# A linear-attention and SwiGLU kernel: first two chunks accumulated over all unit groups, loads limited to two in flight, last pair stored by halves, a new written order

## The chip, the cores and the metric

The kernel runs on one core of a Trainium2 chip. The metric is device time in microseconds (us); the kernel before took 604.38 us, the median of three runs (603.22 to 606.6). A change of about 0.5%, 3 us, is the least that runs of this kernel can tell from none. The engines are named as in the profile: PE multiplies matrices (PEld loads its stationary operand), DVE is the vector engine, ACT the scalar engine, POOL the third elementwise engine, SP the queue that issues most of the transfers (DMAs).

## The reference

Inputs are `r`, `k`, `v` of shape (4, 8, 768, 48), a decay `w` and a bonus `u` of shape (8, 48), and three FFN weights. Per batch and head, a state of 48 x 48 runs over 768 steps; its output is normalised and goes through a gated FFN (384 to 1536 to 384):

```python
for t in range(S):
    cur = einsum('bhd,bhe->bhde', u[None] * k_t, v_t)
    y[:, :, t] = einsum('bhd,bhde->bhe', r_t, state + cur)
    state = w[None, :, :, None] * state + einsum('bhd,bhe->bhde', k_t, v_t)
x = y.transpose(0, 2, 1, 3).reshape(B * S, H * D)
xn = x / sqrt(mean(x * x, axis=-1) + 1e-06) * rms_g
g = xn @ w_gate
out = (g * sigmoid(g) * (xn @ w_val)) @ w_out
```

## The kernel before, in words

**Tiling.** The 768 steps are cut into 12 chunks of 64; with 4 batches, a chunk is 256 tokens. `mixing(s)` (line 788) does the attention of chunk s: products of keys and queries ("E" for chunk 0, "A" later, tile names `chan,ku` and `RR,chan`), a masked copy `MT` on DVE, the outputs Y (`MT,V`, then `RX,ST` and `RR,ST`, which add the state's part), the state update U (`V,KH`), a row of squared sums r (`ones,sq`), and its spread as a diagonal (`diag,ones`). DVE, ACT and POOL build what lies between: decayed queries `RR`, decayed keys in `chan`, `KH`, the norm `ms` and `diag`, and `xa`, `xb`, which are the normalised chunk in two layouts.

**Weights.** They lie in DRAM as 64-bit floats. `quarter(i)` and `piece` (lines 380 to 419 and 972 to 982) load a piece into one of six `raw` buffers (SP), work the low bits on ACT (`ulp`) and DVE (`bits`), and sum on POOL into the 32-bit weights `wa` (gate), `wb` (value) and `wo` (second layer). There are four unit groups; each has two or three pieces of `wa` and of `wb` and two of `wo`, and in the kernel before a group's `wo` follows its `wa` and `wb`.

**The first two chunks** go through the FFN directly while the weights arrive. `gate_val` (line 994) makes one block of units for one chunk: a gate and a value product on PE (12 records each), then a silu on ACT and a multiplication on DVE into `h`. `cell(s, i)` (line 1044) does three such blocks; `add_cell` (line 1024) then projects one unit group through `wo` into a PSUM bank of its own, "P" in this text. The first group's result is copied by ACT into `rows_out`, the next three are added to it by DVE.

**The other ten chunks** go in five pairs. `group(s, m)` makes seven gate and value products for two chunks at a time out of sums of weights and of tokens, six times. `second_layer(s)` (line 1129) makes the projection of a pair out of seven blocks, P1 to P7, each of 24 records on PE, in five half banks: x and w are the two halves of bank a, y is in b, z and v are the halves of c. `plus` adds on DVE, `result` stores. `m1` is ACT's copy of P1's result, made after P1 and before P2 adds to the same half. For the last pair the stores are split between SP's queue and ACT's, and only P3, the last block, is made by halves of the tokens (`js`).

**Order.** Nothing is scheduled by the machine's arrival. Every operation is registered with `Plan.add` with an engine, a cost in us, and the keys that it reads and writes; then `Plan.give` issues all of them in the order of a list of numbers written at the top, `ORDER` (lines 83 to 155). `InOrder` (line 158) keeps that order on every engine; all its instructions have one line in the profile, L166. An engine thus waits at an operation until its inputs are there, with everything that follows queued behind it. `Plan.times` works a start time out of the costs; it is used only by `warm` (line 1082), which puts nine matmuls on ones ahead of the first real product.

**Transfers.** All loads go through SP's queue, in order. A load is issued as soon as SP reaches it and its buffer is free; there is no limit on the number under way. Looks at the raw weights (`check`, line 762) also load through SP, into `rows_out`, in the first and middle part, and count values that the fast path can't take.

**End.** `flag` (line 1203) sums these counts, copies the number into `bad` (DVE, after the last pair's second result row), and all engines load it (L1219) as their last act before a branch (`tc.If`, L1670) over a general kernel that isn't entered here. SP and ACT reach the load only after their last stores.

Of the kernel before, what the change touches and what calls it, by code (L numbers as in the profile page):

```python
# [49 lines left out]
P = 128  # L50
# [22 lines left out]
def feature_order():  # L73
# [10 lines left out]
    0, 5, 1, 14, 9, 4, 6, 49, 3, 16, 2, 19, 54, 11, 8, 17, 15, 12, 50, 51, 53, 24, 55, 10, 57, 52, 20, 56, 59, 29, 84,  # L84
    60, 34, 13, 58, 66, 61, 106, 18, 67, 63, 62, 21, 68, 22, 70, 31, 73, 32, 25, 74, 39, 26, 64, 27, 69, 85, 23, 75,
    65, 7, 91, 71, 76, 72, 28, 77, 109, 86, 96, 78, 139, 36, 44, 37, 79, 140, 142, 97, 114, 30, 87, 92, 80, 143, 88,
    93, 33, 90, 108, 98, 89, 141, 41, 119, 35, 101, 42, 45, 46, 40, 47, 144, 107, 94, 38, 147, 149, 129, 145, 150, 43,
    102, 146, 99, 134, 148, 48, 103, 151, 213, 104, 100, 95, 105, 152, 116, 175, 81, 110, 111, 153, 112, 117, 115,
    154, 113, 120, 155, 124, 176, 118, 156, 82, 222, 157, 171, 158, 83, 159, 166, 160, 216, 121, 167, 161, 122, 172,
    162, 123, 227, 185, 164, 126, 217, 173, 165, 125, 177, 127, 163, 214, 168, 136, 130, 128, 174, 170, 186, 250, 181,  # L90
    187, 218, 219, 182, 188, 131, 132, 178, 183, 135, 137, 259, 195, 184, 242, 247, 260, 179, 196, 248, 232, 180, 133,
    191, 197, 249, 215, 192, 198, 138, 256, 169, 205, 193, 229, 228, 273, 257, 189, 251, 308, 253, 230, 223, 194, 237,
    254, 220, 221, 190, 252, 255, 307, 206, 224, 225, 199, 207, 233, 258, 226, 200, 310, 231, 201, 261, 238, 202, 320,
    234, 208, 235, 274, 209, 354, 262, 210, 236, 211, 203, 275, 265, 266, 263, 212, 355, 357, 267, 358, 283, 268, 356,
    312, 239, 244, 204, 245, 276, 243, 240, 285, 311, 284, 330, 361, 380, 279, 315, 313, 280, 277, 241, 264, 293, 281,
    246, 363, 282, 309, 278, 294, 364, 317, 325, 314, 366, 289, 295, 316, 296, 414, 286, 269, 290, 322, 318, 303, 291,
    360, 292, 319, 359, 367, 326, 413, 362, 299, 331, 327, 328, 287, 304, 321, 365, 300, 323, 567, 301, 368, 305, 288,
    306, 302, 332, 369, 297, 270, 372, 370, 373, 568, 371, 570, 374, 335, 344, 375, 333, 569, 324, 298, 329, 376, 576,
    334, 383, 579, 415, 340, 381, 337, 571, 382, 341, 385, 346, 342, 336, 343, 338, 347, 593, 350, 348, 345, 339, 600,
    580, 384, 351, 387, 388, 393, 352, 353, 394, 377, 349, 400, 395, 577, 396, 390, 401, 272, 412, 404, 402, 271, 403,  # L100
    405, 574, 626, 416, 379, 445, 378, 627, 572, 573, 417, 599, 406, 397, 575, 446, 407, 578, 389, 398, 581, 391, 582,
    408, 411, 583, 585, 586, 594, 419, 628, 587, 453, 409, 418, 410, 447, 454, 399, 588, 421, 449, 448, 424, 455, 629,
    450, 632, 464, 451, 452, 635, 456, 420, 595, 459, 457, 458, 460, 596, 465, 461, 598, 466, 463, 462, 472, 467, 468,
    473, 633, 474, 597, 469, 638, 422, 483, 470, 636, 630, 423, 475, 471, 639, 427, 631, 425, 476, 584, 484, 637, 478,
    601, 485, 479, 392, 480, 491, 482, 486, 487, 492, 477, 493, 481, 488, 428, 502, 489, 426, 490, 430, 494, 652, 659,
    497, 495, 503, 504, 498, 496, 499, 658, 501, 510, 505, 500, 506, 511, 429, 512, 634, 507, 433, 521, 508, 509, 513,
    589, 516, 517, 640, 514, 518, 803, 515, 523, 522, 520, 434, 431, 525, 524, 432, 590, 526, 435, 519, 592, 439, 529,
    527, 436, 528, 532, 530, 804, 591, 531, 535, 642, 533, 540, 536, 537, 539, 542, 541, 534, 544, 641, 543, 538, 545,
    644, 548, 546, 547, 551, 549, 645, 559, 554, 552, 550, 553, 560, 646, 605, 647, 557, 562, 566, 561, 565, 655, 440,
    555, 606, 648, 556, 616, 607, 437, 438, 558, 806, 442, 602, 643, 609, 660, 603, 807, 613, 612, 564, 443, 441, 649,  # L110
    444, 563, 623, 653, 604, 610, 651, 611, 614, 654, 829, 815, 661, 617, 650, 656, 805, 663, 813, 809, 608, 618, 657,
    810, 619, 662, 620, 836, 621, 808, 615, 689, 386, 835, 624, 691, 690, 693, 692, 622, 664, 694, 697, 695, 696, 700,
    698, 625, 812, 699, 703, 701, 811, 708, 704, 862, 705, 710, 709, 668, 707, 816, 665, 712, 711, 702, 814, 713, 863,
    864, 716, 706, 717, 817, 714, 715, 718, 819, 719, 722, 720, 818, 820, 727, 721, 723, 821, 724, 729, 728, 822, 726,
    871, 730, 823, 666, 735, 865, 667, 671, 725, 732, 736, 669, 737, 670, 731, 733, 824, 674, 746, 734, 866, 738, 741,
    739, 747, 742, 832, 743, 748, 830, 745, 740, 750, 749, 869, 744, 751, 831, 672, 754, 752, 673, 753, 757, 755, 834,
    675, 833, 676, 760, 758, 680, 756, 759, 867, 761, 874, 825, 894, 765, 762, 767, 766, 764, 773, 768, 837, 763, 770,
    774, 888, 872, 677, 769, 771, 895, 868, 776, 772, 775, 779, 777, 873, 784, 780, 781, 786, 785, 783, 778, 788, 787,
    678, 826, 681, 789, 679, 782, 682, 683, 792, 790, 875, 791, 686, 795, 793, 870, 798, 796, 797, 799, 876, 828, 794,
    800, 1039, 877, 841, 878, 880, 881, 801, 879, 802, 882, 1040, 842, 852, 1041, 843, 684, 838, 687, 1045, 839, 827,  # L120
    685, 845, 1043, 883, 840, 849, 889, 848, 688, 1042, 1049, 1048, 884, 844, 890, 850, 846, 885, 847, 897, 887, 1052,
    853, 851, 886, 859, 854, 855, 857, 856, 899, 898, 860, 891, 893, 925, 858, 1065, 927, 926, 900, 1072, 933, 928,
    892, 861, 930, 934, 1046, 935, 929, 931, 944, 932, 904, 936, 901, 939, 937, 945, 946, 940, 941, 943, 952, 947,
    953, 1044, 938, 954, 1051, 1071, 942, 949, 948, 950, 955, 951, 896, 1047, 963, 956, 1098, 958, 964, 1050, 902,
    957, 971, 959, 960, 965, 972, 973, 962, 966, 1053, 961, 1099, 1054, 968, 903, 967, 969, 1055, 907, 1057, 982, 970,
    905, 1056, 1100, 974, 1058, 977, 975, 983, 978, 1105, 1059, 984, 1101, 979, 1066, 981, 990, 985, 986, 991, 976,
    992, 1107, 980, 987, 906, 1001, 988, 908, 910, 989, 909, 993, 913, 996, 994, 1002, 1003, 997, 998, 1067, 1000,
    1009, 1004, 995, 1005, 1010, 1060, 1011, 999, 1006, 1020, 1007, 1008, 1012, 1111, 1102, 911, 1015, 1013, 1014,
    1016, 1068, 1021, 1018, 1017, 1073, 1022, 912, 1019, 1124, 1104, 1028, 1023, 1131, 914, 1070, 1024, 1110, 1069,
    1029, 915, 1025, 916, 1030, 1108, 919, 1026, 1103, 1027, 1130, 1031, 1109, 1106, 1034, 1032, 1061, 1033, 1112,  # L130
    1035, 1113, 1077, 1062, 1116, 1114, 1037, 1117, 920, 1275, 1078, 1063, 1118, 1276, 917, 1088, 1079, 1279, 1036,
    918, 1277, 1125, 922, 1038, 1119, 1115, 1074, 1081, 1075, 1278, 1085, 1076, 1287, 1282, 921, 923, 924, 1080, 1082,
    1086, 1126, 1083, 1120, 1064, 1281, 1121, 1084, 1288, 1089, 1122, 1123, 1133, 1285, 1095, 1090, 1091, 1134, 1092,
    1093, 1135, 1136, 1127, 1301, 1161, 1094, 1128, 1163, 1162, 1169, 1164, 1087, 1166, 1170, 1096, 1097, 1165, 1167,
    1137, 1172, 1168, 1308, 1171, 1175, 1173, 1174, 1132, 1180, 1176, 1177, 1179, 1182, 1181, 1140, 1188, 1183, 1178,
    1185, 1189, 1284, 1184, 1186, 1138, 1129, 1191, 1190, 1187, 1199, 1192, 1194, 1200, 1195, 1280, 1196, 1286, 1307,
    1201, 1139, 1198, 1193, 1207, 1202, 1141, 1334, 1142, 1204, 1143, 1208, 1197, 1146, 1203, 1205, 1209, 1210, 1206,
    1283, 1213, 1211, 1214, 1289, 1335, 1215, 1212, 1336, 1291, 1218, 1217, 1220, 1219, 1290, 1222, 1221, 1144, 1216,
    1147, 1223, 1293, 1302, 1226, 1224, 1145, 1294, 1148, 1149, 1225, 1229, 1227, 1152, 1343, 1228, 1232, 1230, 1292,
    1341, 1233, 1295, 1237, 1338, 1234, 1231, 1236, 1239, 1238, 1296, 1241, 1240, 1235, 1242, 1337, 1245, 1303, 1243,  # L140
# [17 lines left out]
class InOrder:  # L158


    def __init__(self, tc, engine):
        self.tc, self.engine = tc, engine
# [6 lines left out]
class Plan:  # L169
# [48 lines left out]
    def give(self, order, free, idle):  # L218
# [3 lines left out]
        for i in order:  # L222
            if self.ops[i][0] == "PE":
                idle(busy, start[i])
                busy = start[i] + self.ops[i][1]
            self.ops[i][3]()
# [1522 lines left out]
```

## Time and profile before

| what | value |
|---|---|
| median of three runs | 604.38 us (603.22 to 606.6) |
| the profiled execution's own time | 606.22 us |
| span of that execution's trace | 604.5 us |
| mean granted PE clock | 0.992 of full speed |
| busy: PE, PEld, DVE, ACT, POOL | 586.1, 512.4, 417.1, 296.3, 42.3 us |
| moved by DMA | 62.99 MB, mean 104 GB/s |
| PE's first matmul, first real product, last matmul's end | 1.15, 10.69, 595.97 us |

The numbers of the page come from one execution, the one of 606.22 us; 1.72 us of it lie outside the span. A row of the timeline gives start and duration of a run of like instructions, and in brackets the idle time before it with what ended it. "issue" means that the engine waited for nothing that the profile shows. Because nearly all instructions have line L166, groups are told apart by tiles: `bank_a<-w,h` is a matmul that writes bank a from a weight sum and h.

### The profile page before, as it was taken

How to read it: one execution, taken by the hardware profiler on the slowest of the kernel's cores; microseconds unless marked ns; L12 is line 12 of the kernel's file. 1: busy time of each engine (PE TensorE's matmuls, PEld its weight loads, DVE VectorE, ACT ScalarE, POOL GpSimd, SP SyncE). 2: the span in 40 equal slices, each digit the busy share in tenths (PEclk: the TensorE clock that was granted, in tenths of full speed). 3: DMA queues.
4: the chain of work that ended last, by engine and by line, in shares of the span. 5: the costliest groups of instructions: out<-in, count | busy, mean ns of one | idle time of the engine just before them, and what ended most of it. 6: DMA issues, size and time to landing. Idle time of an engine off the chain costs nothing.

```text
span 604.5 us, 16467 instructions
## 1 busy us (share of the span) xinstructions
PE 586.1 (97%) x7212; PEld 512.4 (85%) x7212; DVE 417.1 (69%) x622; ACT 296.3 (49%) x721; POOL 42.3 (7%) x40
## 2 busy tenths in 40 slices
PE   8979999999999999999999999999999999999994
PEld 4758778787888999888998888889888899888994
DVE  6859886898777985767875666867666765555631
ACT  6775565756526352574491257555238661123300
POOL 3344332200000000000000000000000000000000
PEclk9899999999999999999999999999999999999997
DMA  7776834223351025115103411511431200201001
GB/s 278 273 269 226 304 112 173 83 79 100 117 176 54 3 80 162 61 54 210 61 6 98 161 35 53 210 34 41 153 125 60 89 12 23 79 2 54 1 14 46
DMA packets 22481, 62.99 MB, mean 104 GB/s; under 512 B 2912, under 2 KB 9728, under 8 KB 20992
## 3 DMA queue, kind: packets, MB, share of 16 engines
q1 hardware_dynamic: 21808, 61.46, 30.3%
q8 instruction: 58, 0.95, 0.6%
q10 hardware_dynamic: 592, 0.39, 0.2%
q14 instruction: 23, 0.19, 0.1%
HBM read 56.04 MB, written 4.72 MB: 101 GB/s over the span
## 4 chain that ended last, share of the span: by engine, by line
PE 95%; DVE 3%; issue 1%; ACT 0%; POOL 0%; DVEq 0%
PE bank_b L166 33%; PE bank_a L166 27%; PE bank_c L166 25%; PE at L166 9%; DVE t L166 1%; DVE MT L166 1%; DVE gv L166 0%; ACT m L166 0%; DVE rows_out L166 0%; DVE ms L166 0%; DVE xa L166 0%; DVE KH L166 0%; POOL ms L166 0%; DVE diag L166 0%; DVE h L166 0%
## 5 line engine op out<-in xcount | busy, mean ns | idle before, releaser
L166 DVE TENSOR_TENSOR gv<-bank_b,m 128x512 f32<-128x512 f32 x90 | 62.2, 691 | 59.2 <-PE bank_b L166 57.3
L166 ACT ACTIVATE gv<-gv 128x512 f32<-128x512 f32 (+1 forms) x60 | 31.1, 522 | 69.0 <-DVE gv L166 68.6
L166 ACT COPY m<-bank_a 128x512 f32<-128x512 f32 (+1 forms) x35 | 19.9, 568 | 78.6 <-PE bank_a L166 62.1
L166 PE MATMUL bank_b<-xa,wa 64*128 64x256 f32 x456 | 56.2, 379 | 0.4 <-DVE gv L166 0.4
L166 DVE TENSOR_TENSOR gv<-bank_c,gv 128x512 f32<-128x512 f32 x60 | 41.4, 689 | 20.2 <-PE bank_c L166 19.7
L166 PE MATMUL bank_a<-wo,h 128*128 128x192 f32 (+1 forms) x264 | 50.7, 346 | 3.7 <-ACT m L166 2.3
L166 PEld LDWEIGHTS bank_a<-wo,h 128*128 128x128 f32 x264 | 43.2, 190 | 8.9 <-ACT m L166 3.5
L166 PEld LDWEIGHTS bank_b<-xa,wa 64*128 64x128 f32 x456 | 43.6, 187 | 6.2 <-DVE gv L166 1.2
L166 PE MATMUL bank_a<-xa,wa 64*128 64x256 f32 x372 | 46.4, 382 | 0.0
L166 PE MATMUL bank_a<-xb,wb 64*128 64x256 f32 x372 | 45.4, 377 | 0.0
L166 PE MATMUL bank_b<-t,s 64*128 64x256 f32 x360 | 44.6, 380 | 0.0
L166 PE MATMUL bank_b<-t,wb 64*128 64x256 f32 x360 | 44.2, 378 | 0.0
L166 PE MATMUL bank_c<-xb,s 64*128 64x256 f32 x360 | 44.0, 377 | 0.0
L166 PE MATMUL bank_c<-t,s 64*128 64x256 f32 x360 | 43.9, 376 | 0.0
L166 ACT ACTIVATE MT<-dmask,du 128x64 f32<-128x64 f32 x160 | 41.5, 338 | 4.4 <-DVE du L166 4.3
L166 ACT ACTIVATE rows_out<-rows_out 128x384 f32<-128x384 f32 x72 | 39.1, 555 | 4.3 <-DMA rows_out<-in_wot_dram 3.7
L166 DVE TENSOR_TENSOR h<-gv 128x256 f32<-128x256 f32 (+1 forms) x60 | 32.7, 550 | 11.0 <-ACT gv L166 10.7
L166 PEld LDWEIGHTS bank_a<-xb,wb 64*128 64x128 f32 x372 | 35.9, 187 | 4.4 <-ACT MT L166 0.3
L166 PEld LDWEIGHTS bank_a<-xa,wa 64*128 64x128 f32 x372 | 35.2, 187 | 4.7 <-issue 0.6
L166 PEld LDWEIGHTS bank_c<-t,s 64*128 64x128 f32 x360 | 34.9, 187 | 4.0
L166 PEld LDWEIGHTS bank_c<-xb,s 64*128 64x128 f32 x360 | 34.8, 187 | 4.0
L166 PEld LDWEIGHTS bank_b<-t,s 64*128 64x128 f32 x360 | 34.3, 187 | 4.5 <-issue 0.3
(177 smaller groups left out, 1070.6 us busy)
## 6 DMA issues: line engine op xcount, KB each, us to landing
chan<-in_chan_dram SPq DMA_DIRECT2D x11, 1024.0 KB, 5.4
TOK<-in_tok_dram SPq DMA_DIRECT2D x10, 768.0 KB, 4.6
V<-in_vpad_dram SPq DMA_DIRECT2D x12, 512.0 KB, 5.2
raw<-in_wot_dram SPq DMA_DIRECT2D x8, 576.0 KB, 5.9
rows_out<-in_wka_dram SPq DMA_DIRECT2D x12, 384.0 KB, 3.3
rows_out<-in_wkb_dram SPq DMA_DIRECT2D x12, 384.0 KB, 3.3
rows_out<-in_wot_dram SPq DMA_DIRECT2D x12, 384.0 KB, 3.6
out_dram<-rows_out SPq DMA_DIRECT2D x43, 96.0 KB, 2.2
```

The source lines that it names most:

```text
L166: return lambda *args, **kwargs: self.tc.keep_in_program_order(give(*args, **kwargs))
```

## The change

- `add_cell` is replaced by `project(s)`. The four unit groups of a first chunk accumulate into one PSUM bank (`start` on the first, `stop` on the last), and ACT copies the finished sum once. All four projections of a chunk stand behind its last `cell` in the program; the pieces of `wo` are registered after all of `wa` and `wb` (`last_weights`).
- `at_most(2, ...)` gives every load of chan, TOK, V and raw on SP's queue a dependency on the landing of the second load before it.
- In the last pair w moves to a bank of `at` and v to the second half of a, and all of P6, P5, P7, P4, P3, the additions and the stores are made by halves of the tokens. `flag()` stands before the last `second_layer`, its cast no longer waits for a result row, and `load`, which loads the flag on all engines, is issued right after the last PE operation of the order.
- Keys name whole PSUM tiles (a, b, c, at) where they named half banks; keys of results name halves. Some costs have new figures. `ORDER` is a new list. The warm-up rule gives four matmuls.

```diff
-    0, 5, 1, 14, 9, 4, 6, 49, 3, 16, 2, 19, 54, 11, 8, 17, 15, 12, 50, 51, 53, 24, 55, 10, 57, 52, 20, 56, 59, 29, 84,
...
+    0, 9, 1, 5, 14, 4, 2, 3, 6, 11, 12, 19, 39, 16, 8, 17, 40, 44, 41, 43, 24, 15, 49, 46, 47, 10, 42, 29, 20, 50, 74,
...
+    def at_most(self, n, give):
+        made = give()
+        self.flying.append(made.ins)
+        if len(self.flying) > n:
+            self.tc.add_manual_dep(
+                made.ins, self.flying.pop(0).name,
+                mybir.DependencyInfo(mybir.DependencyClass.Sync, mybir.DependencyReason.DATA), reason="in flight",
+            )
+        return made
...
-    def give(self, order, free, idle):
+    def give(self, order, free, idle, final):
...
+        last = next(i for i in reversed(order) if self.ops[i][0] == "PE")
...
             self.ops[i][3]()
+            if i == last:
+                final()
...
-        sp.dma_start(out=CH, in_=chan[s])
+        sp.at_most(IN_FLIGHT, lambda: sp.dma_start(out=CH, in_=chan[s]))
...
-    bank_keys = {t: [f"{t}0", f"{t}1"] for t in "abc"}
+    bank_keys = {t: [t, t] for t in "abc"}
...
-        for k in range(2):
-            piece(p, wo[i], wot[i], f"wo{i}.{k}", k * CUT, CUT)
+    def last_weights():
+        for i in range(WQ):
+            for k in range(2):
+                piece(p, wo[i], wot[i], f"wo{i}.{k}", k * CUT, CUT)
...
-    def add_cell(s, i, hs):
+    def project(s):
         po, keys = next_bank()
+        sums, sum_keys = rows_out[:, s], [f"r{2 * s + i}.{j}" for i in range(2) for j in range(2)]
+        for i in range(WQ):
+            def give(i=i, hs=hs_of[s, i]):
+                for j in range(2):
+                    for o in range(NQ):
+                        pe.matmul(
+                            po[:, j, 0:DM], hs[o][0][:, j * P : (j + 1) * P], wo[i][:, o, :], start=i == 0 and o == 0,
+                            stop=i == WQ - 1 and o == NQ - 1,
+                        )
...
+            cells.append(add("PE", 3.87, reads, keys, give, name=f"P {s} {i}", rows="full"))
+        add("ACT", 0.8, keys, sum_keys, lambda: act.copy(sums, po[:, :, 0:DM]), name=f"o {s}")
...
-    cell(0, 3)
+    cell(0, 3), last_weights(), project(0)
...
     cell(1, 3)
-    while waiting:
-        add_cell(*waiting.popleft())
+    project(1)
...
-        if until < 9:
-            for _ in range(int((until - since - 0.6) / 0.9)):
+        if until < 12 and since < 2:
+            for _ in range(int((until - 4.5) / 0.9)):
...
+        last = s + 2 == NS
         keys = {"x": "a0", "w": "a1", "y": "b0", "z": "c0", "v": "c1"}
+        if last:
+            keys |= {"w": "at0", "v": "a1"}
...
+        halves = ((0, 1),) if not last else ((0,), (1,))
+        if not last:
+            mm("z", gs + out_keys("o1"), sum_1, w2(0), True, "P5")
...
+        for js in halves:
+            mm("y", ts + out_keys("o2"), sum_2, w2(1), True, "P6", js)
+            plus(1, ["m1"], "y", None, js, "u2")
+            if last:
+                mm("z", gs + out_keys("o1"), sum_1, w2(0), True, "P5", js)
+            plus(1, [], "z", 1, js, "u4")
+            if not last:
+                mm("w", h_keys[3] + out_keys("o4"), lambda: h[3], w2(2), True, "P4")
+            mm("y", h_keys[1] + out_keys("o3"), lambda: h[1], part(0, 1), False, "P7", js)
+            plus(3, ["m1"], "y", None, js, "u3")
+            if last:
+                mm("w", h_keys[3] + out_keys("o4"), lambda: h[3], w2(2), True, "P4", js)
+            plus(2, [], "w", 3, js, "c21")
+            result(2, s + 1, 0, js)
+            plus(3, [], "z", 3, js, "c22")
+            result(3, s + 1, 1, js)
+            mm("v", h_keys[2], lambda: h[2], part(2, 1), True, "P3", js)
+            plus(1, [], "v", 1, js, "c12")
             result(1, s, 1, js)
...
-        add("DVE", 0.2, [key, "r1"], ["bad"], lambda: dve.tensor_copy(bad, bank[0:1, 0:1]), name="flag")
-        add("ACT", 0.6, ["bad"], [], load, name="flag")
+        add("DVE", 0.2, [key], ["bad"], lambda: dve.tensor_copy(bad, bank[0:1, 0:1]), name="flag")
...
+        else:
+            flag()
         second_layer(s)
...
-    p.give(ORDER, free, warm)
+    p.give(ORDER, free, warm, load)
```

## The prediction, as put on record

> **What bounds the kernel now.** I read the busy shares first, then the slices, then the chain, and from there only the places where TensorE (PE) stands still.
>
> ```profile
> PE 586.1 (97%) x7212; PEld 512.4 (85%) x7212; DVE 417.1 (69%) x622; ACT 296.3 (49%) x721; POOL 42.3 (7%) x40
> PE   8979999999999999999999999999999999999994
> PEclk9899999999999999999999999999999999999997
> PE 95%; DVE 3%; issue 1%; ACT 0%; POOL 0%; DVEq 0%
> ```
>
> PE is busy for 586.1 of 604.5 us and carries 95% of the chain that ended last. Its full-clock work, put together block by block from the durations that recur in undisturbed places (a gate product of 12 records 1.29, an output block of 24 records 3.90, a projection of a first chunk 3.87), is 561.5 us. The span's surplus of 43 us over that is 9.5 us of warm-up matmuls, some 10.5 us lost in the start, the tail of 8.5, the first 1.15, and some 13 in small pieces, the largest 1.7. The change keeps every matmul but five warm-ups, so it can only touch those pieces. In windows of the span (us, length, then PE, PEld, DVE, ACT, POOL busy, granted clock, DMA share, GB/s):
>
> ```profile
> 0.00:10.00 10.00, 8.85 (x17) 3.98 (x18) 6.10 (x26) 6.43 (x20) 1.47 (x12) 1.00 0.75 259
> 10.00:20.00 10.00, 8.95 (x252) 7.20 (x252) 7.43 (x17) 7.01 (x19) 6.15 (x6) 0.90 0.94 346
> 30.00:40.00 10.00, 7.60 (x197) 5.61 (x188) 7.06 (x13) 5.68 (x12) 4.47 (x4) 1.00 0.89 323
> 40.00:50.00 10.00, 9.09 (x70) 7.01 (x68) 5.99 (x14) 8.72 (x18) 3.84 (x4) 1.00 0.70 227
> 50.00:100.00 50.00, 50.00 (x705) 39.92 (x704) 39.42 (x59) 30.04 (x78) 17.13 (x11) 1.00 0.55 196
> 590.00:604.50 14.50, 5.97 (x37) 5.67 (x35) 2.90 (x7) 0.00 (x0) 0.00 (x0) 0.79 0.18 47
> ```
>
> The reader should see that PE's losses end at 50 us and return after 590, and that the DMA engines are nearly full while PE stands. The timeline of PE names three of the holes (start, duration, tile, idle before it and its cause):
>
> ```profile
> 18.11 2.93 PE L166 MATMUL bank_a<-yT,wa 64*128 64x256 f32 x12
> ...
> 36.25 0.25 PE L166 MATMUL at<-RR,ST 48*48 48x64 f32 x1 [2.19 <-issue]
> ...
> 45.33 0.70 PE L166 MATMUL at<-diag,ones 128*128 128x256 f32 x2 [0.91 <-DVE diag L166]
> ```
>
> The first is not a wait: the granted clock is 0.52 in 18 to 20 us, and the product lasts 2.69 to the next block instead of 1.29.
>
> **Part 1, the start: loads two at a time, projections later.** Before, the first ten loads are all issued by 6.33 us and land one per 1.02 us (4.97 to 14.14), each 4 to 8 us after its issue. Loads that fly alone take 3.0 to 3.2 us for 384 KB, 3.27 for 512, 3.7 for 576, 4.36 for 768, 4.70 for 1 MB. After, load n+2 is issued when load n has landed, so two at a time land one per half of these, 1.5 to 1.9 us, if two do not slow each other; I take that, since two at that pace move some 250 GB/s and the trace moved 346. It puts chunk 0's V at 12.8 (before 11.33), chunk 1's channels at 21.0 (17.74), the last raw piece of quarter 0 at 21.3 (14.14), and chunk 1's V at 33.2 (31.56). Each limit is a wait on SP's queue, and SP is in order: the weight loads, chunk loads and stores behind it wait too. VectorE (DVE) waits behind the raw pieces with some 1.9 us, before the first gate products of chunk 0 finish.
>
> The warm-ups fall from 9 to 4 (9.61 us / 18 records, 1.06 each) and end near 5.4, so E starts when chunk 0's r has landed, 9.2, instead of 10.69. The E products, Y, and r follow; Y waits for V at 12.8 as it waited for MT until 12.95; the first gate product comes at 17.3 (18.11). Chunk 1's V and A push: its Y ends at 35.0. Before, the like point (Y of chunk 1 ended) is 37.11. The gain so far is 2.1, and it includes that the 2.19 "issue" hole, in which an instruction transfer of 16 KB is in flight, does not come again. Next, before does a projection (3.97), the r row (1.77) and a gate product that with its wait for the norm's diagonal takes 2.48, and the diagonal's spread. After does gate products there and its r row and spread lie between products, so their waits (1.1 and 0.9) are covered. Work counted: by 45.96 before has done 24.7 us of full-clock work. After lacks of that, at 35.0, one projection 3.87, one r 1.3, one product 1.3, one spread 0.43, so 17.8 are done, and 24.7 are done at 41.9. **Start: 45.96 - 41.9 = 4.1 us gained.** Ends: a loss of 1 (loads 2 us later, the "issue" hole back, 0.69 and 2.19) and a gain of 6 (the half-clock product gone, 1.4, and no wait for DVE).
>
> A page speaks against this part. The Trainium skill, "TensorE: Matmul & The Clock Gate", Part 1, has PE halve its clock after about 3.4 us of idleness and need as long a busy stretch to come back; here PE would stand from 5.4 to 9.2. By that rule E and the sparse blocks after it would run at half clock, about 1 us more; by the trace the first product already pays such a stretch (0.5 granted from 18.10 to 21.51) although nine warm-ups ran, so I add nothing. The sum below does not use the rule.
>
> Once started, 12 gate products of 1.35 and about 7.5 us of attention blocks stand against seven loads per quarter (four pieces of 3.7, then 4.70, 4.36, 3.27: 27.1 us one by one). PE gives them 23.7 us, 3.4 per load, and two at a time need 1.9. So the weights keep ahead, and wo, loaded last, is there near 77 us and wanted near 95.
>
> **Part 2, one accumulation.** Six additions of 128x768 into the rows at 0.95 go, 6 x 0.95 = 5.7 us of DVE; the two ACT copies of 0.8 stay. In 50 to 200 us PE has no idle row, so these lie beside it: worth nothing, at most 0.5 where unit sums come sooner. The eight projections keep their matmuls. A bank is held for four projections, about 16 us; the gate products need the two others, and two banks serve a cell as long as ACT and DVE empty one in the 2.7 us of the next pair of products; their rows are 0.69 + 0.52 + 0.69. Bounds 0 and 1 us of loss; I take 0, since the projections stand together near the end of the stage. If DVE is late, it is a product on the third bank that waits.
>
> PE changes between shapes of tile 94 times instead of 86; a product after a change takes 1.40 against 1.29: 8 x 0.1 = **0.8 lost**.
>
> **Part 3, the second layers.** In three of the middle pairs the block that follows P1 writes the other half of the same bank and waits until ACT has copied m1 out:
>
> ```profile
> 207.47 4.06 PE L166 MATMUL bank_a<-w,h 128*128 128x192 f32 x24
> ...
> 211.57 0.48 ACT L166 COPY m<-bank_a 128x384 f32<-128x384 f32 x1 [4.73 <-PE bank_a L166]
> ...
> 212.10 1.08 PE L166 MATMUL bank_a<-wo,h 128*128 128x192 f32 x5 [0.57 <-ACT m L166]
> ```
>
> From 207.47 the block takes 4.63 to the next, not 3.90: with its drain 0.74. After, P5 or other work stands between, in another bank. Three times: **2.2 gained**. Other holes of the middle (0.57 at 327.7, 0.46 at 399.8, and 1.73 at 389.1, most of it an "issue" wait while an instruction transfer lands) depend on where the new order puts the code: between 0 and 2.8 gained, or as much lost in new places; I take 0. Keys by whole banks add waits only where two halves were in use at once, which is this same place.
>
> **Part 4, the tail.** Before, after PE's last record at 595.97, DVE finishes a full c22 and a half c12, the flag's cast comes behind them, and SP and ACT load the flag only after their last stores:
>
> ```profile
> L1219 SPq TENSOR_LOAD <-bad x1: 879/879/879, 598.5 to 598.5; - x1
> L1219 SPq SEQ_ASSERT  x1: 37/37/37, 599.7 to 599.7; - x1
> L1670 PEldq COMPARE_BRANCH  x1: 4032/4032/4032, 597.5 to 597.5; - x1
> L1670 SPq COMPARE_BRANCH  x1: 45/45/45, 599.8 to 599.8; - x1
> L1670 SPq EVENT_SEMAPHORE  x8: 17/17/17, 602.6 to 603.1; - x8
> ```
>
> From 595.97 to the end are 8.53 us. After, the flag is known and loaded on all engines while PE still works. There is left: the half c12 0.4, one store's issue 0.6 to SP's branch, the 2.77 from SP's branch to its next instruction, and the last 1.93: 5.8 with the short moves. On PE's side the branch (4.03, right after the last matmul) and the 2.9 behind it give 6.9. Between the two I take 6.2: **2.3 gained**, ends 1.5 and 3. The halves on PE cost nothing: two of 1.95 for one of 3.90. The last stores land beside the branch, as they did (601.1 to 601.7).
>
> **Sum.** 4.1 + 2.2 + 2.3 - 0.8 = 7.8 us off a span of 604.5: 596.7. The profiled execution took 606.22, 1.72 around its span, so 598.4 for it. It was 1.84 above the median of 604.38, so a median of 596.6; I say 596.6.
>
> **Rivals.** (a) *Start unchanged.* The later landings eat what the warm-ups and the projections gave. For it: windows 10 to 40 us hold both the full DMA share and the holes. Against it: most holes there are named as DVE, ACT and code, not DMA. 2.2 + 2.3 - 0.8 = 3.7: 600.7.
> (b) *Starved by two in flight, slower.* Place: V and chunk 1's channels before its Y, 17 loads in. My walk has them at 33.2, 1.9 us each. If two slow each other, so that a load takes 2.7 us, V lands near 47, PE stands 14 us longer, 596.6 + 14 = 610.6. It decides (17 x 0.5 us, about the whole gain) from 2.4 us per load on, a quarter to a third longer than mine; one at a time would be 3.1 and more. For it: with eight in flight each took 4 to 8 us, sharing the same queue. Against it: that is 390 GB/s split by eight, and two need 250. The Trainium skill, "DMA: Bandwidth & Descriptors", Anatomy of one DMA, gives each transfer about 2 us fixed beside its bytes; it speaks against few in flight, and the isolated 3.0 to 3.2 us for 384 KB agree with its sum of 2.9.
> (c) *New waits over the whole order.* A new order by new figures may put a bank or a sum late in each of five pairs, at 0.6 to 1.7 each as the rows at 327.7 and 389.1 show: five times 1.3 is 6.5, so 603.1, no change to be measured.
> (d) *More than I count*: the "issue" holes of the start and the middle gone, and the half clock: 4 us more, 592.6.
>
> **Chances.** Mine 0.47, (d) 0.15, (a) 0.15, (c) 0.11, (b) 0.12. What a measurement can tell is 0.5%, 3.0 us: mine, (d) and (a) are faster (0.77), (c) mostly the same (0.11), (b) slower (0.12). Its own range for mine is 592 to 601; eight in ten, leaving out (b) and half of (d)'s far side, 590 to 604.
>
> **What would show it.** Start: loads landing one per 1.5 to 1.9 us, E near 9.2, Y of chunk 1 done near 35, no hole at the r row. If chunk 1's V lands past 40, it is (b). Projections: four in a row on one bank, no DVE addition between. Pairs: no 4.63 us block after P1. Tail: flag loads before the last matmul, 5.8 to 6.9 us from the last matmul to the end. Wrong would be: PE waits for raw or V beyond 50 us, or "issue" waits of over a microsecond in new places.

## The result and the profile after

The changed kernel takes 605.77 us (median of 20 runs, 602.95 to 609.07) beside 605.92 us (20 runs, 602.83 to 609.67) for the kernel before: a ratio of 1.0006 (of the means, 606.14 and 605.78), 95% interval 0.9987 to 1.0025. It is the same time. 596.6 was forecast, with a range from 590 to 604. Every ratio in this text is to the kernel before, run in the same set; it is not the quotient of the two medians.

The page of the changed kernel, one execution of 608.8 us with a span of 607.0. It is one of the longer ones, 3.0 above the kernel's median, while that of before was 0.3 above the median of these 20.

```profile
PE 587.4 (97%) x7202; PEld 516.4 (85%) x7202; DVE 417.9 (69%) x621; ACT 297.1 (49%) x721; POOL 41.3 (7%) x40
PE   5979999999999999999999999999999999999995
PEclk8689999999999999999999999999999999999999
PE 92%; DMA 5%; ACT 1%; issue 0%; SPq 0%; DVE 0%; ACTq 0%
```

The chain, which had no DMA before, now has 5% of it, and the low clock stands in the first three slices (in the second alone before). In windows of its span (us, length, then PE, PEld, DVE, ACT, POOL busy, granted clock, DMA share, GB/s):

```profile
0.00:10.00 10.00, 5.55 (x20) 2.30 (x23) 5.63 (x25) 6.72 (x20) 2.35 (x12) 1.00 0.67 212
10.00:20.00 10.00, 7.50 (x229) 6.83 (x225) 6.71 (x14) 4.95 (x14) 3.74 (x4) 0.57 0.65 205
30.00:40.00 10.00, 7.32 (x199) 5.91 (x188) 9.97 (x15) 7.09 (x12) 3.79 (x3) 1.00 0.82 261
40.00:50.00 10.00, 9.35 (x178) 8.24 (x180) 4.46 (x8) 2.87 (x6) 3.80 (x3) 0.83 0.79 259
50.00:100.00 50.00, 50.00 (x742) 42.77 (x742) 41.43 (x69) 33.05 (x84) 14.48 (x11) 1.00 0.55 183
590.00:607.00 17.00, 10.52 (x65) 10.22 (x63) 2.68 (x8) 0.00 (x0) 0.00 (x0) 0.95 0.13 34
```

In 10 to 20 us the DMA engines moved 205 GB/s, not the 346 of before, and PE was busy 7.50 us instead of 8.95, at 0.57 of its clock. In 50 to 100 us nothing is lost, as before. What PE waited for in the whole span (total, times, longest, us), and then the rows of its timeline behind the waits for transfers:

```profile
PE at L178 <- DMA V<-in_vpad_dram: 4.7, 2, 3.2
PE bank_c L178 <- DMA chan<-in_chan_dram: 3.3, 1, 3.3
PE bank_b L178 <- DVE h L178: 1.1, 1, 1.1
PE bank_a L178 <- ACT m L178: 0.5, 1, 0.5
```

```profile
9.81 0.69 PE L178 MATMUL bank_c<-chan,ku 48*64 48x64 f32 x32 [3.30 <-DMA chan<-in_chan_dram]
...
14.12 1.56 PE L178 MATMUL at<-MT,V 64*64 64x64 f32 x48 [1.46 <-DMA V<-in_vpad_dram]
...
40.65 1.16 PE L178 MATMUL at<-MT,V 64*64 64x64 f32 x64 [3.24 <-DMA V<-in_vpad_dram]
```

8.0 us of waits for transfers stand where before had none. The waits for m1 are nearly gone: 0.5 us in one place, in the last pair, where the view of before has

```profile
PE bank_a L166 <- ACT m L166: 2.3, 4, 0.6
```

At the end of the span (count, duration in ns, start in us) SP has loaded the flag at 578.9 and goes from its last store to the branch:

```profile
L1288 SPq TENSOR_LOAD <-bad x1: 470/470/470, 578.9 to 578.9; - x1
...
L1702 SPq EVENT_SEMAPHORE  x8: 17/17/17, 605.1 to 605.6; - x8
...
L1702 PEldq COMPARE_BRANCH  x1: 3452/3452/3452, 598.0 to 598.0; - x1
...
L1702 SPq COMPARE_BRANCH  x1: 45/45/45, 601.5 to 601.5; - x1
```

The last matmul ends at 600.52, so 6.49 us are left instead of 8.53.

The accounts of three profiles, put together as in the prediction: full-clock lengths of PE's blocks, and what each place took beyond them. "Start" holds the warm-ups and all up to 75 us, "later" the rest up to the last matmul. The first 1.15 us and the last block of 2.1 are the same in all.

| | before | changed | changed, no limit on loads (below) |
|---|---|---|---|
| full-clock work, 0.1 for each change of shape assumed | 561.5 | 562.3 | 562.3 |
| start | 20.6 | 26.6 | 18.3 |
| later | 10.7 | 8.4 | 7.2 |
| last matmul to end | 8.5 | 6.5 | 6.5 |
| span | 604.5 | 607.0 | 597.5 |

Two more kernels below that have the start of the changed one exactly (the two on the flag) took 23.5 and 24.5 in it, with four steps of 3.41 us at half clock instead of the five of this profile, so 26.6 is a high draw; the start lost 3 to 6 us, and the later part and the tail gave 4.3 back.

### The profile page after: what moved, and what is told of

The parts are those of the page before. It is cut to its first block, busy times and chain, and to the rows that moved or that the text cites. A ratio compares the mean times of both kernels' runs of the same rounds, so it can differ in the third digit from the quotient of the medians.

```text
span 607.0 us, 16431 instructions
## 1 busy us (share of the span) xinstructions
PE 587.4 (97%) x7202; PEld 516.4 (85%) x7202; DVE 417.9 (69%) x621; ACT 297.1 (49%) x721; POOL 41.3 (7%) x40
## 4 chain that ended last, share of the span: by engine, by line
PE 92%; DMA 5%; ACT 1%; issue 0%; SPq 0%; DVE 0%; ACTq 0%
PE bank_b L178 32%; PE bank_a L178 26%; PE bank_c L178 24%; PE at L178 10%; DMA V<-in_vpad_dram 2%; DMA chan<-in_chan_dram 1%; DMA raw<-in_wot_dram 1%; DMA raw<-in_wkb_dram 1%; ACT ulp L178 0%; ACT ku L178 0%; ACT wk L178 0%; SPq L178 0%; ACT m L178 0%; DVE MT L178 0%; ACT h L178 0%
## 5 line engine op out<-in xcount | busy, mean ns | idle before, releaser
L178 ACT ACTIVATE gv<-gv 128x256 f32<-128x256 f32 (+1 forms) x60 | 30.7, 521 | 71.9 <-DVE gv L178 71.8
L178 PE MATMUL bank_a<-wo,h 128*128 128x192 f32 x264 | 46.0, 330 | 0.5 <-ACT m L178 0.5
L178 PEld LDWEIGHTS bank_b<-t,wb 64*128 64x128 f32 x360 | 35.2, 187 | 4.8 <-issue 0.9
```

The costliest lines, as they stand in the source:

```text
L178: return lambda *args, **kwargs: self.tc.keep_in_program_order(give(*args, **kwargs))
```

## The experiments

Two theories are set against each other first. Theory A: the limit of two makes the loads so late that PE waits for them. Theory B: the new order of the first 50 us is slow by itself.

**No limit.** The changed kernel with everything else kept.

```diff
-    FIRST, IN_FLIGHT = 2, 2
+    FIRST, IN_FLIGHT = 2, 99
```

> The changed kernel, its order kept, with no limit on loads under way. Theory A (the limit of two starves the start: PE waits 4.7 us for V and 3.3 us for chunk 1's channels): loads land one per about 1.0 to 1.3 us again, V below 12, chunk 1's V below 33, those 8 us of waits shrink to under 2, and the time falls by 5 to 9 us against the changed kernel, to 597 to 601. Theory B (the new order of the first 50 us is itself slow, the landings only show it): the waits move to DVE or ACT and the time stays within 2 us of 605.8.

Measured: 599.82 us beside 605.79 in the same set, ratio 0.9907 (0.9877 to 0.9937). Its windows:

```profile
10.00:20.00 10.00, 8.56 (x218) 7.34 (x212) 7.58 (x19) 8.38 (x24) 5.89 (x6) 0.81 0.87 333
...
30.00:40.00 10.00, 9.97 (x252) 8.72 (x252) 9.93 (x14) 7.72 (x13) 6.71 (x5) 1.00 0.79 265
```

V of chunk 0 lands at 10.98 (13.99 with the limit), chunk 1's channels at 18.09 (24.39), chunk 1's V at 32.02 (40.51); PE waits for no transfer, and 30 to 40 us are full. Theory A holds, B falls: the same order without the limit gives 6.0 us. This kernel is faster than both.

**Three under way.**

```diff
-    FIRST, IN_FLIGHT = 2, 2
+    FIRST, IN_FLIGHT = 2, 3
```

> The changed kernel with three loads under way. Theory A: a load lands per about 1.5 us instead of 2.4, chunk 1's V near 34, most of the waits for V and channels gone, 3 to 8 us faster than the changed kernel. Theory B: within 2 us of it.

600.70 us, ratio 0.9921 (0.9894 to 0.9949); chunk 1's V lands at 33.68. A wait of 1.4 us for V is left, and the time isn't told apart from that without a limit: three are enough.

**The limit alone, on the kernel before.** `at_most` is put around the same loads of the kernel before.

```diff
-    FIRST = 2
+    FIRST, IN_FLIGHT = 2, 2
...
-        sp.dma_start(out=V, in_=vpad[s])
+        sp.at_most(IN_FLIGHT, lambda: sp.dma_start(out=V, in_=vpad[s]))
```

> The kernel before, its order and all else kept, with the limit of two alone. Theory A: the limit by itself costs the start 5 us or more (chunk 1's V lands after 38 us instead of 31.6): 611 to 617. Theory B: at most 2 us, 604 to 608.

614.34 us, ratio 1.0142 (1.0110 to 1.0175). Here PE waits less for loads themselves (0.7 us for V) than for what DVE makes behind them: 3.1 for KH, 2.2 for xa, 2.2 for h. V of chunk 1 lands at 38.27. The limit costs 8.5 us in an order that wasn't written for it, and 6.0 in the one that was.

**The limit from the eleventh load on.**

```diff
-        if len(self.flying) > n:
+        del self.flying[: -n - 1]
+        self.count = getattr(self, "count", 0) + 1
+        if len(self.flying) > n and self.count > 10:
```

> The changed kernel with the limit of two from the eleventh load on; the first ten, up to chunk 1's channels, are issued freely. Theory A, all loads alike: channels land near 18 instead of 24, chunk 1's V near 35 instead of 40, about half of the 6 us between the changed kernel and the one without a limit come back: 602 to 604. If only the first ten matter: 600. If only the later ones do: 605 to 606.

601.66 us, ratio 0.9915 (0.9889 to 0.9941): of the 6 us some 4 come back. Chunk 1's channels land at 20.33, its V at 37.78. The first ten loads carry most of the loss. The 1.8 us that are left against no limit lie within the two intervals, so that the later loads carry the rest isn't shown.

**One under way**, to have each load alone.

```diff
-    FIRST, IN_FLIGHT = 2, 2
+    FIRST, IN_FLIGHT = 2, 1
```

> The changed kernel with one load under way, to have every load's time alone. If a load alone takes what isolated ones took before (3.0 to 3.2 us for 384 KB, 3.7 for 576 KB, 4.7 for 1 MB) and two under way took longer each (3.5, 4.4 to 5.1, 6.8), then two share the bandwidth, and the pace with two is 2.3 us per load instead of the 1.9 of the prediction. One at a time should then pace at 3.3 to 3.9, chunk 1's V should land near 60 us and the kernel should take 620 to 635. If loads alone are as long as those with two, the length is the queue's own and the pace doubles: V past 75, over 640.

651.41 us (two runs), ratio 1.0735 (1.0658 to 1.0813); chunk 1's V lands at 58.91, a pace of 3.39 per load. The time is beyond what was expected, because the losses go on past 75 us, some 32 us beyond the full-clock work against 8.4. The lengths of the loads answer the question. Loads issued in the first 45 us (count, KB each, median us from issue to landing), first one under way, then two (the changed kernel):

```profile
raw<-in_wka_dram SPq DMA_DIRECT2D x3, 384.0 KB, 3.1
raw<-in_wkb_dram SPq DMA_DIRECT2D x3, 384.0 KB, 2.9
raw<-in_wka_dram SPq DMA_DIRECT2D x2, 576.0 KB, 3.7
chan<-in_chan_dram SPq DMA_DIRECT2D x2, 512.0 KB, 3.0
chan<-in_chan_dram SPq DMA_DIRECT2D x1, 1024.0 KB, 4.8
...
V<-in_vpad_dram SPq DMA_DIRECT2D x1, 512.0 KB, 3.5
```

```profile
raw<-in_wka_dram SPq DMA_DIRECT2D x4, 576.0 KB, 4.7
chan<-in_chan_dram SPq DMA_DIRECT2D x2, 1024.0 KB, 6.2
...
raw<-in_wka_dram SPq DMA_DIRECT2D x3, 384.0 KB, 3.5
raw<-in_wkb_dram SPq DMA_DIRECT2D x3, 384.0 KB, 5.2
chan<-in_chan_dram SPq DMA_DIRECT2D x2, 512.0 KB, 4.0
V<-in_vpad_dram SPq DMA_DIRECT2D x2, 512.0 KB, 4.8
```

A load alone is as long as the isolated ones of before. With a second under way the kinds from 512 KB on are 27 to 37% longer; those of 384 KB went from 3.1 to 3.5 and from 2.9 to 5.2. The 17 loads up to chunk 1's V are the same in both kernels, in the same order: from issue to landing they take 57.0 us in sum alone, 3.35 each, and 74.6 with two under way, 4.39 each, 31% more. The first is issued at 1.25 and the 17th landed at 40.51: (40.51 - 1.25) / 17 = 2.31 us per load, where the prediction had 1.88. On average 74.6 / 39.26 = 1.90 were under way, so the pace is 4.39 / 1.90: nearly all of the allowance of two was used, and each load was longer.

**Warm-ups.** Four runs ask what the warm-ups and the low clock are worth. Theory C is that PE's idle time after the fourth warm-up lowers its clock and that this costs time; theory D is that the start waits for data, and that the clock falls in any case. Seven without a limit:

```diff
-            for _ in range(int((until - 4.5) / 0.9)):
+            for _ in range(7):
```

> The changed kernel without a limit and with seven warm-up matmuls instead of four. Theory C (idle PE after the fourth warm-up lowers the clock, and the run without a limit paid for it: E products 0.84 to 1.25 each instead of 0.5, then 0.5 granted from about 17 to 22.5 us): the stretch at 0.5 shrinks or goes, and the time falls by 1.5 to 3 us below the 599.8 of the run without a limit. Theory D (the first 17 us wait for data and the clock is lowered in any case by the many holes between E, A and Y): the half clock stays as it is and the time is within 1 us of 599.8.

601.07 us, ratio 0.9915 (0.9882 to 0.9948), not told apart from 599.82. The stretch at half clock shrank from 6.8 us (16.27 to 23.09) to 3.4 (17.18 to 20.59) and the start from 18.3 to 17.2, but the later part grew from 7.2 to 8.8. So theory C is right on the clock but not on the time: its 1.1 us were given back elsewhere.

Four in the kernel before:

```diff
-        if until < 9:
-            for _ in range(int((until - since - 0.6) / 0.9)):
+        if since == 0.0:
+            for _ in range(4):
```

> The kernel before with four warm-up matmuls instead of nine, nothing else. Its E products then wait only for chan r and ku, some 9.9 us instead of 10.7. If the earlier E is worth something: 0.5 to 1 us faster. Theory C: the idle after the fourth warm-up costs more than that, the half clock comes earlier and lasts longer, and the kernel is 0.5 to 2 us slower.

606.33 us, ratio 0.9998 (0.9968 to 1.0028). E began at 8.7 instead of 10.7, but half clock held from 10.88 to 21.12 instead of 18.10 to 21.51: start 21.0 against 20.6. In these two profiles the two effects cancel.

Nine in the changed kernel, limit kept:

```diff
-            for _ in range(int((until - 4.5) / 0.9)):
+            for _ in range(9):
```

> The changed kernel, limit of two kept, with nine warm-up matmuls. Theory C: of the some 10 us by which its start is later than forecast, the half clock (0.50 granted from 12 to over 24 us in its profile) is 2 to 3, so 603 to 604. Theory A alone: V lands at 14 and the channels at 24 as before, PE waits for them at any clock, and the time stays within 1 us of 605.8.

610.60 us, ratio 1.0062 (1.0037 to 1.0088): 4.8 slower than the changed kernel by the medians (3.4 by the ratios), as no theory had it. In its profile, of an execution of 614.14, the longest of the twelve, 1.5 us lie in the start and 3.7 later. So nine were also run without a limit:

```diff
-    FIRST, IN_FLIGHT = 2, 2
+    FIRST, IN_FLIGHT = 2, 99
...
-            for _ in range(int((until - 4.5) / 0.9)):
+            for _ in range(9):
```

> The changed kernel without a limit and with nine warm-up matmuls. Nine warm-ups under the limit of two were 4.8 us slower than four, which neither theory foretold; in their profile 1.5 us of it lie before 75 us and 3.7 later, most of that in two holes of PE (3.1 us at 248 and 1.3 at 457) that wait for nothing the profile shows, beside an instruction transfer. If more PE instructions ahead shift the places of such holes and lengthen them: holes of 2 us or more return here and the time is 2 to 4 us above 599.8. If the loss belongs to the limit: holes as with four warm-ups (about 1 us) and 599 to 601.

603.24 us, ratio 0.9941 (0.9922 to 0.9959), 3.4 above four warm-ups by the medians (2.1 by the ratios). The start is better than with four, 17.6 against 18.3, and the clock doesn't fall in it, but the later part is 12.0 against 7.2, the same 12.0 as with nine under the limit. Both have the same hole at the same matmul; the rows of PE with nine under the limit, with nine and without it, and then with four and without it:

```profile
250.94 2.23 PE L178 MATMUL bank_c<-t,s 64*128 64x256 f32 x9 [2.01 <-issue]
```

```profile
240.22 1.59 PE L178 MATMUL bank_c<-t,s 64*128 64x256 f32 x9 [2.01 <-issue]
```

```profile
240.25 1.35 PE L178 MATMUL bank_b<-t,wb 64*128 64x256 f32 x10 [0.77 <-issue]
```

A 16 KB transfer of the instruction queue starts at 248.66 in the one and at 238.03 in the other, inside the product in which the hole lies, 248.34 and 237.62. The place of the hole is fixed by a count. Windows from the start of the span to inside the hole, without a limit and with four, seven (a hole of 1.73) and nine warm-ups (us, length, PE busy and its records, granted clock, DMA share, GB/s):

```profile
0.00:240.00 240.00, 234.50 (x3281) 0.99 0.45 156
```

```profile
0.00:239.00 239.00, 234.86 (x3281) 0.99 0.45 157
```

```profile
0.00:239.00 239.00, 234.05 (x3281) 1.00 0.44 157
```

In all three, and in the two kernels under the limit, 3281 records of PE lie ahead of the hole. A warm-up is two records, so each one more moves the hole two records earlier among the products: with seven it comes after 7 records of one product, with nine after 3. Both kernels with nine then have a step at half clock, 251.03 to 254.45 under the limit and 240.98 to 244.39 without; the same window with nine and with four, both without a limit:

```profile
241.00:244.40 3.40, 3.40 (x20) 3.40 (x18) 0.69 (x1) 0.00 (x0) 0.00 (x0) 0.50 0.59 174
```

```profile
241.00:244.40 3.40, 3.40 (x32) 3.04 (x28) 2.31 (x4) 0.63 (x1) 0.00 (x0) 1.00 0.55 175
```

Without a limit, the longer hole (1.2 us), this step (half of 3.41, 1.7) and two more holes near 196 and 448 (1.3) make 4.2 of the 4.8 by which the later part grew. So the loss goes with the number of instructions ahead, not with the limit. Why the hole is longer with more warm-ups stays open: with four it lasted from under 0.2 us (three loads under way) to 1.62 (one under way). That PE waits there for its instructions fits the fixed count and the transfer beside it; no run shows it.

**The tail.** First the loads of the flag alone are put behind everything, its value still early:

```diff
             self.ops[i][3]()
-            if i == last:
-                final()
+        final()
```

> The changed kernel with the flag loaded on all engines behind everything else, as before; its value is still computed before the last second layer. If the early load is what shortened the tail (last matmul to end 6.5 us instead of 8.5), the tail grows back by 1.5 to 2.5 us and the time by as much (607 to 608.5). If the halves of the last pair shortened it, nothing changes (within 0.7 us).

606.37 us, ratio 1.0014 (0.9993 to 1.0036); from the last matmul to the end 6.35 us, against 6.49. By these profiles the early load is worth nothing. Then the value is held back too:

```diff
-        add("DVE", 0.2, [key], ["bad"], lambda: dve.tensor_copy(bad, bank[0:1, 0:1]), name="flag")
+        add("DVE", 0.2, [key], ["bad"], lambda: dve.tensor_copy(given["soon"], bank[0:1, 0:1]), name="flag")
...
     def load():
+        dve.tensor_copy(bad, given["soon"])
```

> The changed kernel (limit of two kept) with the flag's value held back: its cast to bad and the loads on all engines come behind the last result row, as in the kernel before; the halves stay. If knowing the flag early is what shortened the tail by 2.05 us, the time from the last matmul to the end grows from 6.4 to 8 us or more and the kernel by 1.5 to 2 us (607.5). If the halves did it: no change, 605.8.

607.61 us, ratio 1.0017 (0.9992 to 1.0043). The tail is 7.30, between the two: by the profiles, of the 2.05 gained some 0.9 come from the early value. The rest is left for the halves, which no run takes out by themselves. Both intervals hold no change against the kernel before.

**P2 back behind P1.** In the kernel without a limit the order is changed at `give`:

```diff
+            if between and before(copy, second):
+                order = [i for i in order if i not in (copy, second)]
+                k = order.index(first) + 1
+                order[k:k] = [copy, second]
+            elif between and before(*between) and not any(first in self.ops[i][2] for i in between):
+                order = [i for i in order if i not in between]
+                k = order.index(first)
+                order[k:k] = between
...
-    FIRST, IN_FLIGHT = 2, 2
+    FIRST, IN_FLIGHT = 2, 99
```

> The changed kernel without a limit, with P2 put back directly behind P1 and its copy m1 in each of the first four pairs (what stood between goes before P1 or after P2) and the flag's matmul ahead of P1 in the last. If the wait for m1 is worth 0.74 us each, as the blocks after P1 before the change say: 2.5 to 3.5 us slower than 599.8, so 602.5 to 603.5. If other work takes up the gap later: within 1 us.

612.85 us, ratio 1.0088 (1.0058 to 1.0117): 13 above its base by the medians (11 by the ratios), not 3. Some of its rows of PE:

```profile
208.21 4.17 PE L178 MATMUL bank_a<-wo,h 128*128 128x192 f32 x24 [0.57 <-ACT m L178]
```

```profile
406.76 0.70 PE L178 MATMUL at<-sq,ones 128*128 128x256 f32 x2 [1.24 <-ACT last_heads L178]
408.40 5.76 PE L178 MATMUL bank_a<-w,h 128*128 128x192 f32 x24 [0.94 <-ACT rows_out L178]
...
502.28 0.70 PE L178 MATMUL at<-sq,ones 128*128 128x256 f32 x2 [2.60 <-ACT last_heads L178]
```

The waits for m1 come back: 0.57 us of idle time before P2 in each of the four pairs, as in the rows of before. Some 8 us more come with what was moved: the Y that had stood between P1 and P2 no longer does, and the r row and blocks behind it come before ACT and DVE are ready. The rows above show 4.8 us of such waits; and from 408.25 to 411.66 the clock is at half, which stretches the block at 408.40 to 5.76 us, where before has 4.06. Another 3 us are in its start, which the edit doesn't touch: half clock lasted from 12.30 to 25.96 in the profiled execution, four steps instead of two. Of the 12 runs the four with a mean granted clock of 0.989 or more took 608.3 to 610.2 us, the eight below it 612.4 to 614.5. The run shows the wait, and that a move of one block costs more through its neighbours than by itself; it doesn't price the wait alone.

## Why the prediction was wrong

**The step that failed** is in part 1: "two at a time land one per half of these, 1.5 to 1.9 us, if two do not slow each other; I take that, since two at that pace move some 250 GB/s and the trace moved 346". Two do slow each other. The bandwidth over a window of 10 us doesn't say whether two transfers collide while they move their bytes. The term was 1.88 us per load and measured 2.31; by the 17th load that is 7.3 us. The whole of it is the slowing: 1.88 is half of 3.76, which is more than the 3.35 that these loads took alone, but with two under way they took 4.39. By the time alone, 3.0 us at 384 KB and 3.7 at 576, an estimate is that about 2.0 of the 3.7 go with the bytes; that two transfers share this part and not the rest fits 3.7 becoming 4.7, but isn't shown. The forecast gain of 4.1 in the start became a loss of 3 to 6, and without the limit it is a gain of 2.3. Without the limit the rest of this walk comes out: E starts at 8.93 (9.2 forecast), the first gate product at 17.27 (17.3), chunk 1's V lands at 32.02 (33.2) and its Y ends by 35.90 (35.0).

One reading beside it was off, though the sum doesn't use it: the landings from 4.97 to 14.14 before are nine, the tenth load being a small one of 10 KB, so they come one per 1.15 us and not per 1.02.

**Rival (b) had the mechanism** and its point, "from 2.4 us per load on" the whole gain is gone; it was given 12%, and priced at 2.7, so at 610.6. By the prediction's own sign, "If chunk 1's V lands past 40, it is (b)", it is (b): V landed at 40.51. The measured pace lies just short of the point and the time is "the same". The evidence that decided against it, 390 GB/s split by eight, was a rate with many under way, and says nothing on how long one of two takes. The Trainium skill, "DMA: Bandwidth & Descriptors", Anatomy of one DMA, which the prediction names there, states its sum for transfers issued through GpSimd. These loads are SP's; alone, the ones of 384 KB took 2.8 to 3.3 us, near its 2.9.

**The clock** was the second wrong step: "I add nothing". The granted clock falls to half for whole steps of 3.41 us: one before (18.10 to 21.51), two without a limit (16.27 to 23.09), four in the changed kernel (11.36 to 25.02) and one more (42.08 to 45.50) after PE's wait of 3.24 us for V. Windows of the changed kernel on these steps, the last before the fall and the last two at half clock (PE busy and its records, granted clock, DMA share, GB/s):

```profile
7.95:11.36 3.41, 1.08 (x56) 1.00 0.77 252
...
18.19:21.60 3.41, 3.41 (x42) 0.50 0.82 298
21.60:25.02 3.42, 3.42 (x17) 0.50 0.60 218
```

The Trainium skill, "TensorE: Matmul & The Clock Gate", Part 1, has a free-running window of 3.4 us that, idle, halves the clock, and a busy one of the same length that restores it. The length agrees. The rest doesn't quite: from 18.19 to 21.60 PE's records fill the whole step, and the clock still came back only at 25.02; and the windows before a fall weren't idle, with 1.08 us of records before 11.36 here and 2.61 in the 3.41 us before 18.10 in the kernel before. Under the limit the longer stretch is partly covered by the waits for loads; without the limit a stretch of two steps instead of one costs 1.1 in the start, by the profiles with four and with seven warm-ups.

**The r row** of chunk 1 was counted at 1.3, its waits covered by products. They aren't: it takes 1.88 us in the changed kernel, with the limit and without, and 1.77 before. The wait of the diagonal's spread, 0.91 before, is gone as forecast. The r row's 0.6 and the clock's 1.1 are, as far as single profiles tell, about what the start's gain without a limit, 2.3, lacks of 4.1.

**The rest held.** The waits behind P1 are gone in the three middle pairs, 2.2 us as forecast; in the last pair, where only the flag's matmul stands between, 0.51 of the 0.57 us of idle time remain. The text put the wait at the block after P1; it is the block after that, P2, that waits. Three other holes of before, 2.8 together, went, and new ones of 1.15 at 105.9 and 1.02 at 248.4 came (1.08 and 0.75 of them idle time of PE): near the zero that was taken. Later than 75 us 2.3 were gained, against 2.2; that it is so close is partly luck, since without the limit the same part gained 3.5. The tail gave 2.05, against 2.3, but that is luck too: the early load, on which the term was built, gave nothing. The 0.8 for changes of shape is in the account as an assumption and was not measured by itself. Part 2 was not tried by itself, since banks of its own for the late projections would have to be taken from the gate products; in 50 to 100 us PE has no idle in either kernel, so its 5.7 us of DVE bought nothing that the profile shows.

With -0.15 us between the medians the sum is: a start 3 to 6 us worse, 0.8 assumed, 4.3 better behind it.

## What to carry to other kernels

Price a limit on loads under way by loads that run in pairs, not by isolated ones and not by a mean bandwidth: here a second load made 17 loads 31% longer in sum, three under way were enough, and two cost 6 us. Where a kernel starts on data that arrives, write down when each load must land, and count the order of loads as part of the critical chain. A change in several parts can be the same time with one part worth 6 us against it; run each part alone before it is kept.

## What was not expected of the hardware

Five matmuls more at the very start cost 3.4 to 4.8 us by the medians, most of it 200 us later: a hole ahead of the 3282nd record of PE, beside an instruction transfer of 16 KB, grows from 0.8 to 2.0 us, and the clock falls for a step behind it. And the half clock came in whole steps of 3.41 us, before the last matmul's end from one (the kernel before) to five (the changed kernel), and more with one load under way, so that kernels with the same start differ by steps of 1.7 us of PE time. That goes some way to the 6 us over which the runs of one kernel spread: of all runs of the kernel before, those with a mean granted clock of 0.996 or more took 603.0 to 604.6 us, and those with 0.988 or less 608.0 to 611.5. In the 20 of the changed kernel the two go together less.
